# Transposing attention outputs by DMA from SyncE instead of on TensorE

## The chip, the cores and the metric

The kernel runs on one core of one Trainium2 chip. The metric is the device time of one execution in microseconds (us). A run over 1.5% above the fastest of the same kernel counts as slow. The engines are TensorE (PE in the profile, its weight loads PEld), VectorE (DVE), ScalarE (ACT), GpSimd (POOL) and SyncE (SP, which here only issues DMAs). A line number such as L613 is that of the kernel of that run; the change adds five lines, so L621 of before is L626 after.

## The reference, cut to what matters

Masked attention over 4 batches, 8 heads, 768 tokens and head size 64; the heads side by side are the 3072 x 512 input of a mixture of 8 experts.

```
x = attention(q, k, v, proj)          # (4, 8, 768, 64), then to (3072, 512)
P = sinkhorn(exp(x @ w_gate))         # 8 rounds over the whole of x
for e in range(8):
    out += P[:, e:e+1] * (relu(x @ w1[e]) @ w2[e])
```

The products with `w_gate` and `w1` need x with the features on the partitions, so each batch's attention output (tokens on the partitions) is transposed once: four feature blocks of 128, six token tiles of 128 each.

## The kernel before

Attention runs in eight groups (two per batch, four heads each) of 24 units. A unit is two score matmuls, one exponential on ScalarE and six small matmuls with v. While a group runs, SyncE brings the next group's k and q into place, and TensorE gets "filler": the first expert's layers on the batch that is already finished. Cuts are marked with `...`.

```python
# prepare(n): the next group's operands; all of these DMAs are issued by SyncE, in order
def stack(name, h):                 # a head's 64 features, from f16 copies that GpSimd made
    for c in range(2):
        pin(nc.sync.dma_start(out=d[name][32 * c:32 * (c + 1), h, :], in_=t16s[name][...]))
def put_bits():                     # hash bits to DRAM ...
    pin(nc.sync.dma_start(out=dss["kq"]..., in_=bt))
def get_bits(name, h):              # ... and back, into the operands
    pin(nc.sync.dma_start(out=d[name][D:KR, h, :]..., in_=dss["kq"][...]))
# values(): the normalized output of a head, one buffer for a batch
xns[b] = wk.tile([P, J, DD], F16, tag="xn", name="xn", bufs=1)
...
pin(nc.vector.tensor_tensor(xns[b][:, :, c0:c0 + D], nv[:, :, 0:D], rn..., op=Alu.mult))

def turn(b, do):                    # one feature block of one batch
    xp = ops.tile([P, J, P], F16, tag="o", name="xp")
    for j in range(J):
        pin(nc.tensor.transpose(xp[:, j, :], xns[b][:, j, do * P:(do + 1) * P], ident))
    pin(nc.vector.tensor_copy(xT[:, do, b * S:(b + 1) * S], xp.rearrange("p j t -> p (j t)")))

def gate(b): ...                    # 24 matmuls that read all four blocks of xT of batch b
# the loop over units
    if kt == 3 and h % 2 == 0 and u > 5:
        ...
        turn(pb_, pg * 2 + ph // 2)     # a unit with a turn takes no filler
        ...                             # after block 3: fill = filler(pb_, ...), which begins with gate(pb_)
    elif ...
    elif u >= 2 * per:
        ...                             # take filler matmuls
```

The softmax here doesn't subtract the row's maximum and nothing guards it: scores larger than these inputs give would overflow.

Of the kernel before, what the change touches and what calls it, by code (L numbers as in the profile page):

```python
# [20 lines left out]
def kernel(  # L21
# [11 lines left out]
    nc = tc.nc  # L33
    B, H, S, D = q.shape
# [4 lines left out]
    P = 128  # L39
    N = B * S  # L40
    DD = H * D
    DO = DD // P
    FO = F // P
    NBLK = N // P
    J = S // P
# [16 lines left out]
    def pin(ins):  # L62
        tc.keep_in_program_order(ins)
        return ins
# [26 lines left out]
    xT = big.tile([P, DO, N], F16)  # L91
# [484 lines left out]
    av, xns = {}, {}  # L576
# [31 lines left out]
                                        rn.unsqueeze(2).to_broadcast([P, J, D]), op=Alu.mult))  # L608

    def turn(b, do):  # L610
        xp = ops.tile([P, J, P], F16, tag="o", name="xp")
        for j in range(J):
            pin(nc.tensor.transpose(xp[:, j, :], xns[b][:, j, do * P:(do + 1) * P], ident))  # L613
        pin(nc.vector.tensor_copy(xT[:, do, b * S:(b + 1) * S], xp.rearrange("p j t -> p (j t)")))
# [94 lines left out]
    for u in range(len(units) + 1):  # L709
        if u < len(units):  # L710
            n, h, kt = units[u]
            b, g = groups[n]
# [22 lines left out]
        if kt == 3 and h % 2 == 0 and u > 5:  # L735
            pn, ph = (n, h - 1) if h else (n - 1, HG - 1)
            pb_, pg = groups[pn]
            turn(pb_, pg * 2 + ph // 2)
            if pg == NGRP - 1 and ph == HG - 1:
                fill = filler(pb_, J if pb_ < 2 else 2)  # L740
                owed = 0.0
        elif 34 <= u < 43:
            first_part(u - 34 - (u > 39))
        elif u >= 2 * per:
            owed += (total - (8 * 325 if b == 1 else 8 * 865 if b == 3 else 0)) / (2 * per - 8)
            while owed > 0:
                c = next(fill, None)
                if c is None:
                    break
                owed -= c  # L750
                if c == 0:
                    break
# [4 lines left out]
    closing = block(B - 2, 3)  # L757
    next(closing)
    turn(B - 1, DO - 1)
    drain(closing)  # L760
    gate(B - 1)
# [189 lines left out]
```

## Time and profile before

| | |
|---|---|
| time, median of 3 runs | 766.77 us (766.58 to 767.16) |
| TensorE busy | 747.5 us, 98% of the span |
| the nine turns that the change takes away | 54 transposes on TensorE, 9 copies on VectorE |
| attention, up to the last gate | about 208 us of 765.1 |

The busy share tells which engine has work all the time; the chain that ended last tells whose work the end waited for. Here both name TensorE. The lines themselves are in the prediction.

### The profile page before, as it was taken

The page shows a single profiled execution, that of the slowest core. Times are in us where ns is not written, and L with a number is a line of the kernel's source. Part 1 is how long each engine was busy: PE and PEld are TensorE (multiplying, and loading weights), DVE is VectorE, ACT ScalarE, POOL GpSimd, SP SyncE. Part 2 cuts the span into 40 slices and gives each one's busy share as a digit, 9 for nine tenths or more (in the row PEclk, how much of TensorE's full clock was granted, in tenths as well). Part 3 has the DMA queues.
Part 4 walks back from the last instruction along what each step waited for, and adds up shares of the span by engine and source line. Part 5 has one row for each costly group of instructions (what it writes and reads, how often), then busy time and mean ns, then how long its engine had stood idle before and what let it go on. Part 6 is the DMA issues. An engine that isn't in the chain of part 4 may idle for free.

```text
span 765.1 us, 16738 instructions
## 1 busy us (share of the span) xinstructions
PE 747.5 (98%) x6294; PEld 517.2 (68%) x6294; DVE 567.4 (74%) x1261; ACT 514.0 (67%) x1027; POOL 318.3 (42%) x327
## 2 busy tenths in 40 slices
PE   8999999999999999999999999999999999999997
PEld 3655566566654677777777777777777777777664
DVE  6787666667579777777777777777777777777774
ACT  6986786678655777766666666666666666666661
POOL 6766353449200433443344334433543344324222
PEclk9999999999999999999999999999999999999999
DMA  8779447841030464776477648754964496443335
GB/s 227 203 195 227 126 128 174 175 124 27 2 56 8 83 108 80 125 126 115 90 130 132 112 84 144 121 95 83 171 118 90 91 165 112 84 84 83 84 77 145
DMA packets 41569, 88.08 MB, mean 115 GB/s; under 512 B 7232, under 2 KB 21840, under 8 KB 41488
## 3 DMA queue, kind: packets, MB, share of 16 engines
q0 software_dynamic: 27168, 69.49, 46.9%
q1 hardware_dynamic: 13324, 16.48, 8.2%
q10 hardware_dynamic: 996, 1.05, 0.6%
q8 instruction: 49, 0.80, 0.5%
q14 instruction: 32, 0.26, 0.1%
HBM read 53.05 MB, written 7.08 MB: 79 GB/s over the span
## 4 chain that ended last, share of the span: by engine, by line
PE 84%; DVE 6%; ACT 6%; issue 1%; DMA 1%; SPq 0%; ACTq 0%; DVEq 0%
PE a L829 18%; PE a L250 18%; PE d L829 13%; PE y L250 9%; PE st L570 6%; PE d L250 4%; ACT pt L573 4%; PE hp L647 4%; PE yp L662 3%; PE num L586 3%; PE pr L406 1%; PE hp L325 1%; PE yp L309 1%; ACT acc L241 1%; DVE hT L838 1%
## 5 line engine op out<-in xcount | busy, mean ns | idle before, releaser
L838 DVE CUSTOM_DVE_ANT_0 hT<-d,u 128x384 f16<-128x384 f32 x336 | 185.5, 553 | 96.2 <-ACT u L834 94.7
L254 ACT ACTIVATE vt<-a,p 128x256 f32<-128x256 f32 x324 | 153.3, 473 | 148.7 <-PE a L250 148.3
L834 ACT COPY u<-a 128x384 f32<-128x384 f32 x336 | 160.8, 479 | 23.5 <-PE a L829 19.9
L573 ACT ACTIVATE pt<-st 128x768 f16<-128x768 f32 x192 | 147.1, 809 | 42.5 <-PE st L570 41.8
L289 POOL DMA_DIRECT2D acc<-vt x72 | 62.0, 861 | 267.1 <-ACT vt L254 114.0
L250 PEld LDWEIGHTS <-hT 128*128 128x128 f16 x1296 | 126.3, 97 | 50.4 <-DVE hT L838 0.9
L250 PE MATMUL a<-t,hs 128*128 128x256 f16 x972 | 145.8, 273 | 2.2 <-ACT vt L254 1.0
L250 PEld LDWEIGHTS <-hs 128*128 128x128 f16 x972 | 94.8, 98 | 38.5 <-issue 2.8
L829 PEld LDWEIGHTS <-t 128*128 128x128 f16 x896 | 87.7, 98 | 36.4 <-issue 0.6
L829 PE MATMUL d<-xd,t 128*128 128x384 f16 x448 | 109.4, 326 | 0.3 <-DVE hT L838 0.3
L829 PE MATMUL a<-xT,s 128*128 128x384 f16 x448 | 109.4, 326 | 0.2
L570 PE MATMUL st<-qs,ks 71*128 71x384 f16 x384 | 94.0, 325 | 3.6 <-ACT pt L573 2.4
L250 PE MATMUL y<-t,hT 128*128 128x256 f16 x648 | 97.1, 272 | 0.0
L258 DVE SCALAR_TENSOR_TENSOR acc<-y,p,acc 128x256 f32<-128x256 f32 x162 | 77.4, 478 | 11.4 <-PE y L250 11.4
L134 POOL TENSOR_TENSOR t<-t 128x1024 f16<-128x1024 f16 (+1 forms) x39 | 81.9, 2108 | 0.1
L586 PEld LDWEIGHTS <-pt 128*128 128x128 f16 x1152 | 60.5, 97 | 25.9 <-ACT pt L573 0.4
L829 PEld LDWEIGHTS <-s 128*128 128x128 f16 x672 | 65.5, 98 | 17.5 <-issue 2.5
L586 PE MATMUL num<-va,pt 128*128 128x65 f16 x1152 | 66.5, 193 | 0.3 <-ACT pt L573 0.3
L868 ACT ACTIVATE hT<-a 128x384 f16<-128x384 f32 x112 | 54.0, 482 | 1.8 <-PE a L829 1.7
L829 PE MATMUL a<-xd,s 128*128 128x384 f16 x224 | 54.3, 323 | 0.8 <-ACT u L834 0.8
L829 PE MATMUL d<-xT,t 128*128 128x384 f16 x224 | 54.7, 326 | 0.0
L829 PE MATMUL a<-xT,t 128*128 128x384 f16 x224 | 54.7, 326 | 0.0
(121 smaller groups left out, 948.7 us busy)
## 6 DMA issues: line engine op xcount, KB each, us to landing
acc<-vt POOLq DMA_DIRECT2D x72, 512.0 KB, 4.8
t<-in_moe_w_dram POOLq DMA_DIRECT2D x26, 512.0 KB, 8.5
v<-in_v_dram POOLq DMA_DIRECT2D x28, 192.0 KB, 5.7
out_dram<-acc SPq DMA_DIRECT2D x78, 64.0 KB
acc<-in_k_dram POOLq DMA_DIRECT2D x6, 768.0 KB, 7.1
acc<-in_q_dram POOLq DMA_DIRECT2D x6, 768.0 KB, 12.2
t<-in_moe_w_dram POOLq DMA_DIRECT2D x3, 1024.0 KB, 12.0
ks<-t SPq DMA_DIRECT2D x60, 48.0 KB
```

The lines of the kernel that those rows point to most:

```text
L134: pin(nc.gpsimd.tensor_tensor(o[:, sl], x[:, sl], y[:, sl], op=op))
L250: pin(nc.tensor.matmul(dst, hq[hn][:, fo, :], wq[wn][:, fo, :], start=first and fo == 0, stop=fo == FH - 1, skip_group_check=True))
L254: pin(nc.scalar.activation(out=vt[:, k], in_=a, func=Act.Copy, scale=p))
L258: pin(nc.vector.scalar_tensor_tensor(out=dst, in0=src, scalar=p, in1=dst, op0=Alu.mult, op1=Alu.add))
L289: pin(nc.gpsimd.dma_start(out=acc[:, b, i], in_=vt, accum_op=Alu.add))
L570: pin(nc.tensor.matmul(st[:, i, 0:HT], d["k"][0:KR, h, kt * P:(kt + 1) * P], d["q"][0:KR, h, i * HT:(i + 1) * HT], start=True, stop=True))
L573: pin(nc.scalar.activation(out=pt, in_=st[:, :, 0:HT], func=Act.Exp, scale=scale))
L586: pin(nc.tensor.matmul(num[:, j * (D + 1):(j + 1) * (D + 1)], pf[:, j * P:(j + 1) * P], va[:, h, kt, :], start=(kt == 0 and j == 0), stop= ...
L829: pin(nc.tensor.matmul(bk, wq[wn][:, do, f * P:(f + 1) * P], xq[xn][:, do, :], start=first and do == 0, stop=do == 1, skip_group_check=True))
L834: pin(nc.scalar.copy(t, bk))
L838: pin(add(TENSOR_ADD_SAT, out=dst, in0=bk, in1=u, s0=3e38, s1=0.0))
L868: pin(nc.scalar.activation(out=hT[:, f, hi], in_=a, func=Act.Relu))
```

## The change

Its intent is to take 54 of TensorE's matmuls, and VectorE's copies after them, off the engines that work hardest, and to let the DMA engines do the transposes. Block 3 of each batch, the last one before the gate, stays on TensorE, as does all of batch 0.

```diff
     def turn(b, do):
+        if b and do < DO - 1:
+            for j in range(J):
+                pin(nc.sync.dma_start(out=xT[:, do, b * S + j * P:b * S + (j + 1) * P],
+                                      in_=xns[b][:, j, do * P:(do + 1) * P], transpose=True))
+            return
         xp = ops.tile([P, J, P], F16, tag="o", name="xp")
```

## The prediction

> **What bounds the kernel now.** I read the page first: busy shares, then the chain that ended last. After that I read busy time by stage, the transposes by tile, and SyncE's queue in order of time.
>
> ```profile
> PE 747.5 (98%) x6294; PEld 517.2 (68%) x6294; DVE 567.4 (74%) x1261; ACT 514.0 (67%) x1027; POOL 318.3 (42%) x327
> ...
> PE 84%; DVE 6%; ACT 6%; issue 1%; DMA 1%; SPq 0%; ACTq 0%; DVEq 0%
> ```
>
> TensorE is busy for 98% of the span and holds 84% of the chain; DMA holds 1% and SyncE's sequencer (SPq) rounds to 0%. So work taken off TensorE counts, if nothing else steps onto the chain. The change lies in the attention stage, which I cut at about the borders of its eight groups (two per batch, about 26 us each; groups 3 to 6 below):
>
> ```profile
> core 0: us, PE busy (x) PEld busy (x) DVE busy (x) ACT busy (x) POOL busy (x), PEclk, DMA share, GB/s
> ...
> 81.00:107.00 26.00, 25.70 (x278) 15.38 (x276) 16.02 (x30) 19.36 (x27) 12.17 (x19) 1.00 0.46 130
> 107.00:133.00 26.00, 25.43 (x302) 16.75 (x301) 18.50 (x36) 18.75 (x25) 12.21 (x19) 1.00 0.69 172
> 133.00:160.00 27.00, 26.75 (x288) 15.98 (x287) 17.71 (x32) 19.16 (x26) 12.88 (x20) 1.00 0.69 162
> 160.00:186.00 26.00, 25.37 (x318) 17.16 (x316) 19.80 (x35) 20.76 (x29) 19.10 (x24) 1.00 0.29 73
> ```
>
> TensorE is busy 25.4 to 26.75 of each 26 to 27 us, ScalarE and VectorE 16 to 21. All are TensorE-bound at full clock, and the DMA engines are already 29 to 69% busy.
>
> The transposes by tile:
>
> ```profile
> L613 PE MATMUL xp<-ident,xn x96: 216/219/229, 28.0 to 206.2; 128*128 128x128 f16 x96
> L614 DVE COPY xT<-xp x16: 511/558/559, 28.5 to 206.4; 128x768 f16<-128x768 f16 x16
> ```
>
> There are 16 turns (4 batches of 4 feature blocks) of six 128x128 transposes and one copy. The 219 ns is latency: they are pipelined.
>
> SyncE's queue is what the change loads:
>
> ```profile
> 82.19 5.69 SPq L400 DMA_DIRECT2D ks<-t  x4
> 88.18 3.88 SPq L400 DMA_DIRECT2D qs<-t  x4
> 94.64 0.35 SPq L422 DMA_DIRECT2D ds<-bt  x1
> 95.03 2.17 SPq L400 DMA_DIRECT2D ks<-t  x2
> 100.17 0.28 SPq L425 DMA_DIRECT2D ks<-ds  x1
> 100.48 0.30 SPq L425 DMA_DIRECT2D qs<-ds  x1
> ...
> 106.93 0.31 SPq L425 DMA_DIRECT2D qs<-ds  x1
> 107.43 4.44 SPq L400 DMA_DIRECT2D ks<-t  x4
> 111.97 2.44 SPq L400 DMA_DIRECT2D qs<-t  x4
> 119.57 0.35 SPq L422 DMA_DIRECT2D ds<-bt  x1
> ```
>
> In every group SyncE brings the next group's k and q into place: stacks of 32 partitions, then the hash bits out to DRAM and back. A plain issue takes 0.3 to 0.6 us, and the queue runs from 82.19 to 107.24: nearly the whole group, its last issue 0.2 us before the next group's first. It is in order, so anything put into it delays what follows. The next group's first scores run at about 106; their bits are issued at 100.2.
>
> The nearest reader of the transposed data, after the turn on the feature block that stays on TensorE:
>
> ```profile
> 108.84 0.50 PE L613 MATMUL xp<-ident,xn 128*128 128x128 f16 x6
> ...
> 111.24 0.74 PE L621 MATMUL lg<-wg_sb,xT 128*128 128x8 f16 x24
> ```
>
> The gate at 111.24 reads all four blocks of batch 1, and TensorE is in order too.
>
> **What the Trainium skill says.** "VectorE: DVE Perf Modes", section "The three transpose paths", lists a 128x128 bf16 transpose at 390 ns on TensorE and 1309 ns by DMA. The trace's TensorE form is 219 ns of latency. The kernel before has no DMA transpose, so no row here tests the 1309 ns. "DMA: Bandwidth & Descriptors", section "Latency and other measured facts", gives DMA_TRANSPOSE an effective 261 GB/s, which for one 32 KB block would be 0.13 us: the two disagree by ten unless small transposes are bound by something other than bandwidth. Section "Anatomy of one DMA" of that page gives about 2 us fixed cost per DMA, mostly the receipt; in the trace the store of the bits issued at 94.64 holds its readers until 100.17, 5.5 us, under load. Section "Issuing engines are not separate DMA queues" says that all DMAs share the same 16 engines, so the transposes also meet the loads issued by GpSimd.
>
> **The change part by part.** Removed: 9 turns (batches 1 to 3, blocks 0 to 2), or 54 matmuls and 9 VectorE copies. From the start of a turn to the next scores TensorE moves on by 0.33 us (196.0 to 196.32) or 0.43 (136.14 to 136.57), so 9 x 0.35 = 3.2 us off the binding engine, 0.4% of the span. The copies (9 x 0.56 = 5 us) are off VectorE, which isn't the bound. Nothing else in TensorE's order moves.
>
> Added: 54 DMA transposes in SyncE's queue, six per turn. The order of the instructions shows where. Blocks 0 and 1 of a batch come into the same preparation: six ahead of the k stacks and six between the k and q stacks, during groups 3 and 5. Block 2 comes at the end of that preparation's queue, ahead of the next group's k stacks. New waits: the gate on the landings, and VectorE's first normalized write of the next batch (one buffer) on all the transposes that read the old one.
>
> Let c be SyncE's time (or the transposes' own pace, whichever is slower) per transpose. I choose c = 1.3 from the 1309 ns, so six take 7.9 us. Working in the time of before:
> - Group 3. The queue is free at 81.4. 81.4 + 7.9 + 5.7 (k) + 7.9 + 3.9 (q) = 106.8 for the store of bits, against 94.64: 12.1 late. The bits for the next scores were issued at 100.2, with 2 us to land, for use at 106.2: slack 4. TensorE stalls 8.1.
> - Gate of batch 1. The preparation ends at 107.2 + 12.1 = 119.3; six more end at 127.2 and land at 129.2. The gate stands at 111.2 + 8.1 = 119.3: stall 9.9.
> - Group 4's preparation carries only those six; its store of bits waits anyway for the hash (queue idle 114.4 to 119.57, 5 us). No stall.
> - Group 5. Free at 132.9: 132.9 + 7.9 + 4.4 + 7.9 + 3.9 = 157.0, against 146.35: 10.6 late, slack 4.9 (bits issued at 152.5, used at 159.4): stall 5.7.
> - Gate of batch 2 (163.74): 160.7 + 10.6 + 7.9 + 2 = 181.2 against 169.4: stall 11.8.
> - Batch 3: no preparation is left in group 7. Three turns from 179.3 end at 203.0 and land at 205.0, before the gate at 207.1: no stall.
>
> Sum: 8.1 + 9.9 + 5.7 + 11.8 = 35.5, less 3.2: 32 us, or 799 us. Idle of one stall may be partly shared with the next (VectorE and ScalarE catch up, the filler work is spread by count), so I take 3 us off: 796.
>
> **The rivals.**
> 1. Transposes issue like plain copies (c about 0.43). The same sum gives six in 2.6 us, group 3 late by 1.5 (covered), the gates stalled 2.1 and 1.6: +3.7 - 3.2, so 767. For it: the 261 GB/s and plain issues of 0.3 to 0.6 us. Against it: the 1309 ns. Even then there is no gain, because the queue ends a preparation at 107.2, only 4 us ahead of the gate. With c = 0.6 the gates stall 5.1 and 4.7: 773; with c = 1.0 the sum is 24.3: 788. The 2% line (782) is at about c = 0.85.
> 2. All hidden, only the 3.2 us remain: 763.5. It needs c below about 0.3; the plain store of the bits, also 128 rows, takes 0.35 in the rows above.
> 3. A transpose is cut into small pieces and costs twice the 1309 ns or more, or waits behind GpSimd's loads (DMA share 0.69). With c = 2.9, the stalls at groups 3 and 5 are 27 and 25, at the gates 19 and 21, at the last gate 26: 118 us, so about 880. For it: small descriptors, and the 5.5 us of the loaded store. Against it: nothing measured.
> 4. VectorE's wait on the buffer is the stall, not the gate: it comes within 1 us of the gate (the write is at 112.85), so the time is the same, and only the name of the waiter differs.
>
> **Range and chances.** Above 0.6 the sums give some 40 to 50 us of time per us of c. I give c below 0.85 about 0.27, and between 0.85 and 2.2 about 0.6. Predicted 796 us, range 770 to 845 for 8 in 10. Faster by over 2% can't come out of 3.2 us: 0.02. Within 2%: 0.25. Slower by over 2%: 0.73.
>
> **What would show it.** SPq rows of the transposes with six per turn in about 7.9 us; the store of the bits in groups 3 and 5 late by over 10 us; TensorE idle before the first scores of groups 4 and 6, put down to the DMA of ks or qs, and before the two gates, put down to xT or xn; busy time of TensorE down by about 54 matmuls and the time after attention (from the last gate to the end, 558 us) unchanged. It is wrong if the issues are as short as plain ones, if the stalls sit only at the gates, or if the later stage changes.

## The result

The changed kernel is correct and takes 797.72 us (median of 4 runs, 793.24 to 800.23) against 766.95. The ratio is 1.0397, with a 95% interval of 1.0362 to 1.0433. Ratios are the mean time of one kernel's fast runs over that of the other's of the same rounds, so they are not quite the ratio of the medians quoted. All four runs are fast ones; their granted TensorE clock is 0.973 to 0.980, against 1.000 in the profiled run of before. The profiled execution of after is the quickest of the four.

The page of the changed kernel, busy times and chain:

```profile
PE 753.2 (95%) x6240; PEld 518.5 (66%) x6240; DVE 560.3 (71%) x1252; ACT 514.8 (65%) x1027; POOL 317.8 (40%) x327
...
PE 80%; DVE 6%; ACT 6%; DMA 4%; SPq 3%; issue 1%; ACTq 0%; DVEq 0%
```

TensorE has 54 matmuls fewer and yet 5.7 us more busy time: its matmuls ran slower. DMA and SyncE's sequencer, at 1% and 0% of the chain before, now hold 7% of it.

The stage in which it happens, from 80 us to just after the last gate, before and then after. The columns are the stretch, its length, busy time and count for PE, PEld, DVE, ACT and POOL, the granted clock, the DMA share and GB/s:

```profile
80.00:208.00 128.00, 125.72 (x1444) 79.79 (x1443) 85.74 (x155) 94.77 (x126) 67.02 (x88) 1.00 0.44 111
```

```profile
80.00:234.60 154.60, 130.82 (x1383) 80.98 (x1382) 80.06 (x147) 94.07 (x125) 66.28 (x88) 0.90 0.45 103
```

What follows, from there to the end of the traces at 765.0 and 791.0, is as long as before (557 and 556.4). The whole loss is in attention: 154.6 - 128 = 26.6 us. TensorE's idle time there rises from 128 - 125.7 = 2.3 to 154.6 - 130.8 = 23.8, by 21.5 us; its busy time rises by 5.1, at a granted clock of 0.90. The sum is the 26.6.

SyncE's queue in group 3 of the changed kernel, start and length in us:

```profile
80.13 7.96 SPq L613 DMA_TRANSPOSE xT<-xn  x6
88.20 2.56 SPq L400 DMA_DIRECT2D ks<-t  x4
90.87 8.45 SPq L613 DMA_TRANSPOSE xT<-xn  x6
99.42 2.44 SPq L400 DMA_DIRECT2D qs<-t  x4
101.96 0.53 SPq L422 DMA_DIRECT2D ds<-bt  x1
...
111.05 7.52 SPq L613 DMA_TRANSPOSE xT<-xn  x6
```

Six transposes hold the queue for 7.5 to 8.5 us. The queue now has no gap (the rows left out are the plain issues of the operands); the store of the bits (`ds<-bt`) comes at 101.96 in place of 94.64, and block 2 is issued only from 111.05. TensorE's side of it:

```profile
106.07 0.49 PE L570 MATMUL st<-qs,ks 71*128 71x384 f16 x2 [1.76 <-DMA qs<-ds]
...
116.36 0.64 PE L626 MATMUL lg<-wg_sb,xT 128*128 128x8 f16 x8 [3.11 <-DMA xT<-xn]
...
122.05 0.27 PE L626 MATMUL lg<-wg_sb,xT 128*128 128x8 f16 x4 [1.91 <-DMA xT<-xn]
124.03 0.22 PE L626 MATMUL lg<-wg_sb,xT 128*128 128x8 f16 x2 [1.72 <-DMA xT<-xn]
```

In brackets is the idle time before a group and what ended it. The next group's first scores wait 1.76 us for their bits. The gate of batch 1 then takes one token tile after the other as it lands, and idles 3.11 + 0.80 + 1.80 + 1.91 + 1.72 = 9.3 us (two of the five are cut). In batch 2 the same two places idle 2.44 and 6.8 us.

The clock around these waits:

```profile
106.10:111.20 5.10, 4.84 (x48) 3.49 (x49) 3.06 (x5) 3.92 (x5) 1.75 (x3) 0.67 0.25 65
111.20:124.50 13.30, 3.34 (x49) 2.29 (x48) 3.58 (x7) 2.46 (x4) 9.24 (x15) 0.63 0.98 212
124.50:140.00 15.50, 15.46 (x144) 9.09 (x144) 8.48 (x16) 8.46 (x11) 1.50 (x3) 0.88 0.33 106
```

After the short wait the granted clock falls to 0.67 while TensorE is busy, and after the gate it is still 0.88 on average over 15 us. These are averages of two values: cut at its steps, the trace shows 0.50 from 107.82 to 111.24 and from 114.65 to 128.30, and 1.00 before, between and after. So each of these waits is followed by slow matmuls.

### The profile page after: what moved, and what is told of

The parts are those of the page before. It is cut to its first block, busy times and chain, and to the rows that moved or that the text cites. A ratio compares the mean times of both kernels' runs of the same rounds, so it can differ in the third digit from the quotient of the medians.

```text
span 791.5 us, 16682 instructions
## 1 busy us (share of the span) xinstructions
PE 753.2 (95%) x6240; PEld 518.5 (66%) x6240; DVE 560.3 (71%) x1252; ACT 514.8 (65%) x1027; POOL 317.8 (40%) x327
## 4 chain that ended last, share of the span: by engine, by line
PE 80%; DVE 6%; ACT 6%; DMA 4%; SPq 3%; issue 1%; ACTq 0%; DVEq 0%
PE a L834 18%; PE a L250 17%; PE d L834 12%; PE y L250 9%; PE st L570 5%; PE d L250 4%; PE hp L652 4%; ACT pt L573 3%; PE num L586 3%; SPq L613 2%; PE yp L667 2%; DMA xT<-xn 1%; PE hp L325 1%; PE yp L309 1%; ACT acc L241 1%
## 5 line engine op out<-in xcount | busy, mean ns | idle before, releaser
L570 PE MATMUL st<-qs,ks 71*128 71x384 f16 x384 | 97.1, 334 | 8.9 <-ACT pt L573 3.7
L586 PEld LDWEIGHTS <-pt 128*128 128x128 f16 x1152 | 62.3, 99 | 27.7 <-issue 2.9
L586 PE MATMUL num<-va,pt 128*128 128x65 f16 x1152 | 68.2, 196 | 0.3 <-ACT pt L573 0.3
L570 PEld LDWEIGHTS <-ks 71*128 71x128 f16 x384 | 34.0, 100 | 32.4 <-issue 13.1
## 6 DMA issues: line engine op xcount, KB each, us to landing
t<-in_moe_w_dram POOLq DMA_DIRECT2D x3, 1024.0 KB, 12.1
```

The source lines that it names most:

```text
L570: pin(nc.tensor.matmul(st[:, i, 0:HT], d["k"][0:KR, h, kt * P:(kt + 1) * P], d["q"][0:KR, h, i * HT:(i + 1) * HT], start=True, stop=True))
L586: pin(nc.tensor.matmul(num[:, j * (D + 1):(j + 1) * (D + 1)], pf[:, j * P:(j + 1) * P], va[:, h, kt, :], start=(kt == 0 and j == 0), stop= ...
```

## The experiments

Theory Q: the cost is the time that the issue of a transpose takes in SyncE's in-order queue, at the places where something behind it or its own landing has a deadline. Rival N: a DMA transpose costs about the same wherever it stands (31 us over 54). A further question is whether the removed TensorE work was worth the predicted 3.2 us at all; theory H, also told as rival H, says that it was not, because the turns stood in units that ScalarE paces. The runs of before that shared the chip had medians of 766.7 to 767.4.

**1. Block 2 alone** (`block2`)

```diff
-        if b and do < DO - 1:
+        if b and do == DO - 2:
```

> Only feature block 2 of batches 1 to 3 is transposed by DMA (18 transposes), blocks 0 and 1 stay on TensorE. Theory Q (place in SyncE's queue against a deadline): the preparations before it are punctual again, but block 2 is still issued after them, so six transposes at 1.24 us end at 114.7, land about 5.4 us later at 120.1, and the gate of batch 1 due at 111.2 stalls 8.9 us; the gate of batch 2 stalls 9.5; the clock loses some 2 us after each; 1 us saved on TensorE: about 788 us. Rival N (each DMA transpose costs the same wherever it stands, 31 us over 54 of them): 18 of them, +10 us, 777 us.

Measured: 788.23 us, ratio 1.0276 (1.0258 to 1.0294). Theory Q had 788, rival N 777. The bits are punctual again (94.53), the transposes go out from 106.80, and both gates wait, 7 us in all for batch 1 (and 8 for batch 2). Theory Q had 8.9 and 9.5, so its hit on the total is partly luck. One third of the transposes brings two thirds of the loss.

**2. Blocks 0 and 1 alone** (`block01`)

```diff
-        if b and do < DO - 1:
+        if b and do < DO - 2:
```

> Only feature blocks 0 and 1 are transposed by DMA (36 transposes), block 2 back on TensorE. Theory Q: no gate waits any more, only the late hash bits of groups 4 and 6 (1.8 and about 4.5 us of stall as in the changed kernel, about 1.5 us of clock each), 2.1 us saved: about 773 us. Rival N: 36 transposes, +21 us, 787 us.

Measured: 780.32 us, ratio 1.0181 (1.0154 to 1.0207): between the two, nearer to theory Q. As it said, no gate waits for a landing; the only waits are those of the first scores of groups 4 and 6 for their bits, but they are longer than in the changed kernel (there 1.76 and 2.44), and part of the first one lies on k's stack besides (the profiled run, 784.34 us, is the slowest of the four):

```profile
PE st L570 <- DMA ks<-ds: 3.6, 1, 3.6
PE st L570 <- DMA qs<-ds: 2.9, 1, 2.9
```

The granted clock falls to 0.75 and 0.70 in the 20 us around them. So the expectation was right on the place of the loss and too low on its size, by some 7 us.

**3. The places that looked free** (`free`) and **4. batch 3 alone** (`batch3`)

```diff
-        if b and do < DO - 1:
+        if b and do < DO - 1 and (b == B - 1 or do == 0):     # free
+        if b == B - 1 and do < DO - 1:                        # batch3
```

> Block 0 of batches 1 and 2 and blocks 0 to 2 of batch 3 by DMA (30 transposes). Theory Q: block 0 alone fits ahead of the k stacks (queue free at 81.4, six end at 88.9, k and q stacks by 94, the bits are due at 94.6), and after batch 3 no preparation follows; no new wait, 5 turns of 0.35 us saved: 765.0 us, 0.2% faster. Rival N: 30 transposes, +17 us, 784 us.

> Only batch 3 (18 transposes, blocks 0 to 2). Theory Q: no preparation follows in the queue; blocks 0 and 1 early, block 2 issued at about 196 and landed at 196 + 7.5 + 3 to 5 = 206.5 to 208.5 against a gate at 207.1: 0 to 1.5 us of stall less 1 us saved, 766 to 767.5 us. Rival N: +10 us, 777 us.

Measured: `free` 766.33 us, ratio 1.0002 (0.9978 to 1.0026); `batch3` 767.05, ratio 1.0005 (0.9990 to 1.0019). Rival N, with 784 and 777, falls: 30 and 18 transposes cost nothing that these runs can show where nothing behind them is due. (In the profiled run of `free`, 769.89 us, the first scores of group 6 do wait 1.03 us for their bits, which the expectation had ruled out.) In `batch3` all 18 go out in one row and no gate waits for them:

```profile
180.29 24.50 SPq L613 DMA_TRANSPOSE xT<-xn  x18
```

But the gain that was expected is missing too: neither interval holds a gain of more than 0.22%. TensorE's order around block 2 of batch 3 tells why at that place; before, and then `batch3`:

```profile
195.48 0.48 PE L570 MATMUL st<-qs,ks 71*128 71x384 f16 x2 [0.26 <-ACT pt L573]
...
195.99 0.50 PE L613 MATMUL xp<-ident,xn 128*128 128x128 f16 x6
196.32 0.49 PE L570 MATMUL st<-qs,ks 71*128 71x384 f16 x2
...
197.70 0.49 PE L570 MATMUL st<-qs,ks 71*128 71x384 f16 x2
```

```profile
195.61 0.49 PE L570 MATMUL st<-qs,ks 71*128 71x384 f16 x2 [0.26 <-ACT pt L573]
...
196.31 0.48 PE L570 MATMUL st<-qs,ks 71*128 71x384 f16 x2
...
197.68 0.49 PE L570 MATMUL st<-qs,ks 71*128 71x384 f16 x2
```

The turn filled 0.33 us between two units. Without it, from one score start over the next to the one after, 2.22 us (195.48 to 197.70) became 2.07 (195.61 to 197.68): 0.15 us won, not 0.33. The rest was waiting time. The unit has no filler, and ScalarE's exponentials there run back to back; this line of before has four of them in 3.10 us, which is the pace that TensorE had to keep (in `batch3` the same four take 2.96):

```profile
194.62 3.10 ACT L573 ACTIVATE pt<-st 128x768 f16<-128x768 f32 x4 [0.38 <-PE st L570]
```

**5. The turns left out** (`drop`): one cheap plain copy per turn in place of the transposes, with a wrong result.

```diff
-            for j in range(J):
-                pin(nc.sync.dma_start(out=xT[:, do, ...], in_=xns[b][:, j, ...], transpose=True))
+            pin(nc.sync.dma_start(out=xT[:, do, b * S:(b + 1) * S], in_=xT[:, do, 0:S]))
```

> The nine turns are left out altogether: in place of six transposes SyncE issues one plain copy per turn of batch 0's block (wrong result on purpose; about 0.35 us of queue each). It shows what the removed TensorE and VectorE work was worth. As predicted (0.35 us per turn): 3.2 us faster, 763.6 us. Rival H (a turn stands in a unit that has no filler and that ScalarE's exponentials pace at 0.81 us, so TensorE waits there anyway): no gain, 766.5 us.

Measured: median 765.62 us against 766.97, ratio 0.9997 (0.9973 to 1.0021; one of the six runs took 771.51, the other five 764.85 to 766.19). By the medians the removed work was worth 1.35 us; by the interval at most 0.27%, or 2.1 us. Both are below the predicted 3.2. That 1.35 is also 9 x 0.15 is chance. Comparing score starts around each of the nine turns in the traces of before and `drop`, as above, gives for blocks 0 to 2: batch 1, 0.33, 0 and 0; batch 2, 0.34, 0 and 0.33; batch 3, 0, 0.12 and 0.15: 1.27 us in all. So three turns were worth their full 0.33, two a part, and four nothing. At each of those four places `drop` has a wait of 0.26 or 0.27 us for ScalarE's exponentials that the kernel before does not have (85.67, 99.05, 135.69 and 173.38). One of the four is the turn at 136.14 that the prediction had read as 0.43. So theory H holds in full for four turns and in part for two. By these numbers some 1.3 us is all that taking the nine turns off TensorE could win in this order of work.

**6. and 7. Idle matmuls during the gate's wait** (`warm`, `warm2`), to keep the clock up:

```diff
+        if b in (1, 2):
+            wt = ops.tile([P, 512], F32, tag="o", name="wt")
+            for _ in range(36):        # warm2: 20
+                pin(nc.tensor.matmul(wt, tiny, tiny.unsqueeze(1).to_broadcast([P, 4, P]), start=True, stop=True))
         gate(b)
```

> The changed kernel with 36 idle matmuls of 0.216 us (7.8 us) in TensorE's order ahead of the two gates that wait (10.5 and 7.6 us in the profile). Theory K (part of the loss is the lower clock granted after the idle time): clock back near 1.00 after the gates, TensorE busy falls, 3 to 5 us faster than the changed kernel, 793 us. Rival (the waits alone are the loss): the same time as the changed kernel, 797 to 798 us, or longer where the idle matmuls outlast the wait.

> As the run with idle matmuls, but 20 in place of 36, because the profile of that run showed them at the lower clock (0.53 granted, some 0.43 us each), where 36 outlasted the wait. Theory K (the lower clock after the waits costs time of its own): 20 of them fit into the waits of 10.5 and 7.6 us, the clock is back at 1.00 when the gate is done, and 2 to 4 us are won: 794 us. Rival: no change, 797 us.

Measured: 796.55 us (ratio 1.0386, 1.0369 to 1.0404) and 798.38 (1.0395, 1.0366 to 1.0424): no change from 1.0397. Both are inconclusive. In `warm` the wait of batch 1's gate is covered (0.3 us left) and the clock was 1.00 from 120 us until the next wait for bits. But the idle matmuls themselves ran at the low clock that the wait for the bits had left (0.53 from 111 to 120), and that wait was 3.39 us in this profiled run against 1.76; the gate's exponential came at 126.97 in place of 124.28. The waits differ from run to run by as much as the clock could win. In `warm2` the idle matmuls ran out early, and the clock was 0.76 from 120 to 130. That the lower clock lengthens TensorE's work is in the trace of the changed kernel; that it can be bought back in this way is not shown.

**8. Half the rows per transpose** (`halves`)

```diff
-                pin(nc.sync.dma_start(out=xT[:, do, ...128 columns], in_=xns[b][:, j, ...], transpose=True))
+                for r in range(2):
+                    t0 = b * S + j * P + r * 64
+                    pin(nc.sync.dma_start(out=xT[:, do, t0:t0 + 64],
+                                          in_=xns[b][64 * r:64 * (r + 1), j, do * P:(do + 1) * P], transpose=True))
```

> Each 128-row transpose cut into two of 64 rows (108 in all). If the issue costs by rows (128 packets of 256 bytes each), one half takes about 0.62 us and the time stays near 797 us. If it costs by the instruction, each half takes 1.23 us, a turn holds the queue for 15 us, and by the sum of the prediction the time goes past 840 us.

Measured: 858.63 us (one run, state unknown). A turn of twelve holds the queue for 15 to 17 us; the median issue of half the rows takes 1.227 us, that of the whole 1.231. The cost is by the instruction, not by the rows.

```profile
81.19 16.62 SPq L615 DMA_TRANSPOSE xT<-xn  x12
```

**9. From ScalarE's queue** (`act`)

```diff
-                pin(nc.sync.dma_start(out=xT[:, do, ...], ..., transpose=True))
+                pin(nc.scalar.dma_start(out=xT[:, do, ...], ..., transpose=True))
```

> All 54 transposes issued from ScalarE's queue. If the issue holds the issuing engine for 1.23 us as on SyncE, ScalarE loses 7.4 us per turn, its exponentials stop and TensorE with them: nine stalls of some 6 us, over 50 us, about 820 us and SyncE's stores of bits punctual (94.6, 146.4). If a queue only costs its own order, SyncE's queue is free again and the gates wait little: 770 us or less.

Measured: 857.79 us (one run, state unknown), so the first reading, and worse than its 820. ScalarE issues six in 7.58 us and starts no exponential in that time:

```profile
97.48 7.58 ACTq L613 DMA_TRANSPOSE xT<-xn  x6
105.16 1.51 ACT L573 ACTIVATE pt<-st 128x768 f16<-128x768 f32 x2 [6.95 <-DMA xT<-xn]
```

The issue holds whichever engine makes it. The expectation's stalls of some 6 us were short: TensorE stops at every one of the nine turns for 6.2 to 10.7 us, and the clock falls with it (0.947 over the whole run). Whether SyncE's stores of bits were punctual in themselves can't be read from this run, since everything else had moved.

**10. A second buffer for the attention outputs** (`twobuf`)

```diff
-                xns[b] = wk.tile([P, J, DD], F16, tag="xn", name="xn", bufs=1)
+                xns[b] = (spool.tile([P, 3, 2, F // 2], F16, tag="s1", name="xn").rearrange("p a b f -> p (a b) f") if b % 2
+                          else wk.tile([P, J, DD], F16, tag="xn", name="xn", bufs=1))
```

> A second buffer for the attention outputs (every other batch in a buffer that is free at that time), so that VectorE's first write of a batch no longer waits for the transposes of the batch before (9.7 and 6.9 us of wait in the changed kernel). If that wait binds: 10 us or more faster, 785 us. If the gate binds at the same moment, as predicted: VectorE's wait is gone and the time is the same, 796 to 798 us.

Measured: 796.59 us, ratio 1.0382 (1.0351 to 1.0414). VectorE's wait for the transposes is gone and the time is the same within the intervals: the gate alone is enough to hold the time.

**11. One instruction per turn** (`wide`): the attention outputs are kept as (block, token tile, feature), so that a whole turn is a two-dimensional transpose of 128 x 768.

```diff
-                xns[b] = wk.tile([P, J, DD], F16, tag="xn", name="xn", bufs=1)
+                xns[b] = wk.tile([P, DO, J, P], F16, tag="xn", name="xn", bufs=1)
...
-            pin(nc.vector.tensor_tensor(xns[b][:, :, c0:c0 + D], ...))
+            pin(nc.vector.tensor_tensor(xns[b][:, c0 // P, :, c0 % P:c0 % P + D], ...))
...
-            for j in range(J):
-                pin(nc.sync.dma_start(out=xT[:, do, ...], in_=xns[b][:, j, ...], transpose=True))
+            pin(nc.sync.dma_start(out=xT[:, do, b * S:(b + 1) * S].rearrange("p (j t) -> p j t", j=J),
+                                  in_=xns[b][:, do].rearrange("p j c -> p (j c)"), transpose=True))
```

> The attention outputs are kept block by block (block, token tile, feature), so that one instruction transposes a whole turn: 128 rows by 768, nine instructions in place of 54, the same bytes. Theory I (a fixed cost of about 1.23 us per instruction, as the halves suggest, which cost 1.227 each for half the rows): a turn holds the queue for 1.3 us, bits and gates are punctual, 765.5 to 766.5 us. Rival C (the issue costs by the columns, 128 of them 1.23 us): a turn holds the queue for 7.4 us in one piece, and the time stays at 790 to 800 us.

Measured: correct, 768.20 us, ratio 1.0025 (0.9990 to 1.0061); the six runs go from 766.84 to 775.72. The queue:

```profile
87.54 1.24 SPq L612 DMA_TRANSPOSE xT<-xn  x1
94.21 0.35 SPq L422 DMA_DIRECT2D ds<-bt  x1
107.11 2.16 SPq L612 DMA_TRANSPOSE xT<-xn  x1
119.15 0.36 SPq L422 DMA_DIRECT2D ds<-bt  x1
```

The same bytes in nine instructions instead of 54 cost 1.24 us each where they didn't wait, no more than one of 128 x 128. The bits are punctual (94.21 against 94.64 before), the gate waits for nothing, and the profiled span is 765.1 us, as before. The packets are the same too: both traces have 6912 of 256 bytes, so neither the bytes nor the number of packets makes the loss by itself. This undoes the loss and keeps the change: theory Q holds with the issue as its cost. It wins nothing all the same: the nine turns give back the same 1.27 us here, but in this trace the first scores of group 6 wait 1.01 us for k's stack, for which there was no wait before; what delayed that stack is not shown.

**12. Filling the freed places** (`widefill`): as `wide`, and the units from which a turn was taken now take filler too.

```diff
+        turned = False
         if kt == 3 and h % 2 == 0 and u > 5:
             ...
             turn(pb_, pg * 2 + ph // 2)
+            turned = pb_ == 0 or pg * 2 + ph // 2 == DO - 1
             ...
-        elif 34 <= u < 43:
+        if turned:
+            pass
+        elif 34 <= u < 43:
             ...
-            owed += (...) / (2 * per - 8)
+            owed += (...) / (2 * per - 5)
```

> The whole-turn transposes, and the units that TensorE's turns had occupied now also take their share of the filler matmuls (in the other kernels the unit with a turn takes none). Theory H (the nine turns stood where ScalarE's exponentials set the pace, so taking them out alone frees nothing): only with those slots filled does the removed work count, at most 9 x 0.35 = 3.2 us, so 764 to 765 us, 0.2 to 0.4% faster than before. Rival: the filler is bounded elsewhere, no change from the whole-turn kernel, 766.5 to 768 us.

Measured: correct, median 772.11 us, ratio of the fast runs 1.0047 (1.0006 to 1.0088), with runs from 766.32 to 778.17; the slowest, the profiled one, counts as slow and is not in the ratio. The expected gain did not come, and rival and theory are both missed. In the slow profiled run TensorE waits 1.74 us for k's stack at 55.6, ahead of all DMA transposes, and 3.27 us for bits at 165.0, and its clock falls after both; I don't build on that run. Why these runs scatter more is open.

No version beats the kernel before.

## Why the prediction was right, and where it was not

The predicted time was 796 us in a range of 770 to 845, "slower" with a chance of 0.73; it is 797.72. The mechanism was the predicted one. Among its terms several were off, and they cancel in part, so the closeness of the total is partly luck.

- *c = 1.3 us per transpose, from the skill's 1309 ns.* Right: the median issue takes 1.231 us. But I took it for the pace of a 128 x 128 block. `halves` and `wide` show that it is per instruction from 64 x 128 to 128 x 768. The prediction's third rival, small pieces that cost by their number, is in this sense out; its other half, data that wait behind GpSimd's loads, came true in part (see the gates).
- *The stalls at groups 4 and 6, 8.1 and 5.7 us.* Right place, mis-sized: 1.76 and 2.44. I counted the k and q stacks at 5.7 and 3.9 us, as before, but much of that was waiting for GpSimd's copies. Coming later they took 2.56 and 2.44, so the bits were 7.3 us late, not 12.1. And at group 4 the store of the bits let its readers go after 1.8 us, not 5.5. At group 6 that took 7.0 us (6.2 before); there the stacks took 2.71 and 2.45 in place of 4.4 and 3.9, and SyncE came to the transposes only 9.4 us later than before (142.27 against 132.9), while TensorE ran 13.4 us or more behind all through that group. The slack was misread besides: the first scores of the two groups start at 105.25 and 157.80 in the trace of before, not at 106.2 and 159.4; this alone would have made the stalls longer.
- *The stalls at the gates, 9.9 and 11.8 us.* Measured 9.3 and 6.8. The first is near for two errors that cancel: the queue was less late, and the landing took longer than 2 us. In the trace the last transpose of batch 1's block 2 was issued by 118.57 and its last packet ended at 123.29, 4.7 us later, while the DMA share was 0.98. (The section "Anatomy of one DMA" from which the prediction took its 2 us is about DMAs issued by GpSimd; these are SyncE's, and the trace has both 1.8 and more than 4.7 us for them.) At the second gate the sum had the queue 4.9 us further behind than TensorE; it was 0.8: its preparation ended 17.8 us later than before (178.45 against 160.70), and TensorE came 17.0 later (180.74 against 163.74).
- *No stall at the last gate.* Right: 18 transposes are issued by 231.03, the gate at 233.2 waits for none.
- *3.2 us saved on TensorE.* Wrong. The failed step is "9 x 0.35 = 3.2 us off the binding engine": I took the engine that binds the stage for the one that binds each unit. `drop` puts it at 1.35 us by the medians, and the traces at 1.27: six of the nine turns gave back less than their 0.33 us, because ScalarE set the pace at their places.
- *Rival 4, that VectorE's wait for the buffer is the stall, not the gate.* Not so: the trace puts TensorE's 9.3 and 6.8 us down to the gate's reads of xT, and in `twobuf` the wait for the buffer is gone without any gain. That the time would be the same was right.
- *Missing altogether: the clock.* TensorE's busy time in the stage rose by 5.1 us although work was taken away; the prediction's sign "busy time down by about 54 matmuls" failed. The Trainium skill, "TensorE: Matmul & The Clock Gate", Part 1, has an idle TensorE fall to half its clock until it has been busy for a while; the trace agrees in kind (half the clock from 107.82 to 111.24 and from 114.65 to 128.30, both after waits).

The sum as it stands: the four stalls measure 1.8 + 9.3 + 2.4 + 6.8 = 20.3 us in the profile (predicted 35.5), the idle total rose by 21.5, the slower clock added 5.1 net of the removed work, and the profiled run was 4.5 us below the median of the four.

## What to carry to other kernels

A DMA issue is work on an in-order queue: before putting transfers there, count instructions times the issue time, look up what stands behind them and when it is due, and first make the instructions larger rather than the transfers fewer. Work removed from the busiest engine is worth only what its own place shows: here six of the nine turns stood where ScalarE set the pace in whole or in part. Where a wait is unavoidable, count the slower matmuls after it too.

## What the Trainium skill lacked or had wrong

- "VectorE: DVE Perf Modes", "The three transpose paths": 1309 ns for a 128 x 128 DMA transpose is about right as the issue time (1.231 us here), but the page does not say that it is per instruction: 64 x 128 took 1.227 us and 128 x 768 took 1.24 us.
- "DMA: Bandwidth & Descriptors", "Issuing engines are not separate DMA queues", calls the time to initiate a DMA usually small relative to the DMA itself. For a 128 x 128 transpose it is the other way round: 1.23 us of issue for 0.27 us of packets, and the issuing engine does nothing else meanwhile (ScalarE: six in 7.58 us, with no exponential started between).
- The same page, "Latency and other measured facts", gives 261 GB/s for DMA transposes, measured on one kernel. In the trace a 32 KB block is 128 packets of 256 bytes, which without other traffic took 0.27 us from first start to last end, 121 GB/s, and a 196 KB turn took 1.10 us, 179 GB/s; beside GpSimd's loads the data lagged its issue by up to 4.7 us.
- "TensorE: Matmul & The Clock Gate", Part 1, table of states: the lower clock comes there after at least one idle window of about 3.4 us. Here half the clock was granted from 107.82 to 111.24, and in the 3.41 us before that TensorE was still busy for 1.49 us; the longest single wait in them was 1.76 us. So less than a whole idle window was enough.
